# Another order of the first phase, and 28 products that nothing reads, in a kernel of attention and a two-layer FFN

## The chip, the cores and the metric

One core of a Trainium2 chip runs the kernel. The time is that of the device for one execution, in microseconds (us). The engines are TensorE (PE; its weight loads stand apart as PEld), VectorE (DVE), ScalarE (ACT), GpSimd (POOL) and SyncE (SP, which here issues all the DMAs).

## What is computed

```
attention, for each of 8 batches and 8 heads (576 positions, 64 wide):
  q_d, k_d, v_d = means over 4 neighbouring positions          # 144 positions
  out_d   = softmax(q_d k_d^T / 8) v_d                          # pooled part
  scores  = q k^T / 8 where |i - j| < 4, else -1e9
  out     = repeat(out_d, 4) + softmax(scores) v                # local part
x = out as 4608 tokens x 512
h = x w_in                                                       # 512 x 2048
g = h where h >= 1;  0 where h <= -1;  (h + 1)^2 / 4 between
result = g w_out                                                 # 2048 x 512
```

## The kernel before

**Work units.** Attention goes by pairs of heads, four pairs to a batch: pair n is one run of the generator `attention(n, pool)`, cut by `yield` into nine pieces. For a pair, PE makes the local scores (`sl_ps`, L179 and L191) and the pooled scores (`sp_ps`, L226); DVE takes maxima (L210, L242, L243) and subtracts (L211); ACT makes the exponentials, `sl` in place at L218 and `sp` in three parts at L246; DVE sums, inverts and scales both in place (L255 to L261); PE transposes them (`tl_ps` L280, `tp_ps` L292); ACT copies these out (`al`, `ap`); PE multiplies by v (`pl_ps` L324, L336); ACT and DVE put the two parts together (`xd` L345, `x` L347), and ACT and POOL split x into a rounded part `xh` (L358) and its rest `xl` (L359).

**The FFN** takes 512 tokens (`c`) and 128 hidden columns (`f`) at a time. `mm1` makes `h_ps` in 12 products (L463) and the activation behind it (`u`, `gh`, `gl`); `mm2` adds 12 products to four `o_ps` banks (L499). There are 9 x 16 such steps of each. The weights arrive as 512 KB blocks (`raw_i`, `raw_o`), and `convert_weights` (step `c`) makes each of them usable: two passes on ACT (L381, L383), two on DVE (L386, L387, both into `m`), a rounding on ACT (L389) and a subtraction on POOL (L390).

**Order.** Two tables are written out by hand. `BEFORE_STEPS` runs the first batch (pairs 0 to 3, and the first pieces of pair 4's loads); then `FIRST_STEPS` mixes the FFN's first steps (`s` is an `mm1`, `m` an `mm2`) with pairs 4 to 7; a loop does the rest. In a table `a2` is the next piece of pair 2, `q3` loads pair 3's q and k, `v` loads the first v, `w` loads one block of w_in and one of w_out, and `c` converts one block. A scheduler turns this order into one queue for each engine, which the engine works off in order, with waits on semaphores.

**Buffers.** While the first batch runs, four PSUM tiles of two banks go round over all of `sl_ps`, `sp_ps`, `tl_ps`, `tp_ps` and `pl_ps`; from pair 4 on there is one. `sl` has two buffers. Ten products of an identity matrix by itself (`warm`, L433) stand at the very start.

## Time and profile before

| | |
|---|---|
| median of 3 runs | 999.39 us (997.0 to 999.83) |
| the profiled execution | 999.97 us |
| its span on the chip | 998.2 us |
| PE busy | 966.9 us, 97% |
| DVE / ACT / POOL busy | 389.2 / 456.4 / 370.0 us |
| mean granted clock of TensorE | 0.978 |

The span runs from the first to the last instruction; the 1.8 us between it and the execution's time lie around it. [...]

### The profile page before, as it was taken

The page shows a single profiled execution, that of the slowest core. Times are in us where ns is not written, and L with a number is a line of the kernel's source. Part 1 is how long each engine was busy: PE and PEld are TensorE (multiplying, and loading weights), DVE is VectorE, ACT ScalarE, POOL GpSimd, SP SyncE. Part 2 cuts the span into 40 slices and gives each one's busy share as a digit, 9 for nine tenths or more (in the row PEclk, how much of TensorE's full clock was granted, in tenths as well). Part 3 has the DMA queues.
Part 4 walks back from the last instruction along what each step waited for, and adds up shares of the span by engine and source line. Part 5 has one row for each costly group of instructions (what it writes and reads, how often), then busy time and mean ns, then how long its engine had stood idle before and what let it go on. Part 6 is the DMA issues. An engine that isn't in the chain of part 4 may idle for free.

```text
span 998.2 us, 16966 instructions
## 1 busy us (share of the span) xinstructions
PE 966.9 (97%) x7036; PEld 765.2 (77%) x7036; DVE 389.2 (39%) x644; ACT 456.4 (46%) x911; POOL 370.0 (37%) x309
## 2 busy tenths in 40 slices
PE   5699999999999999999999999999999999999998
PEld 4577777777777777777777777777777788888886
DVE  5978795333333333333333333333333311111110
ACT  3889444444454444443443444444444443334333
POOL 1556665333333333333333333333333322222222
PEclk7679999999999999999999999999999999999999
DMA  8695111211121112111121112111211010001001
GB/s 292 222 325 167 51 49 50 83 34 50 50 91 40 35 50 92 49 50 50 62 80 49 29 48 92 49 41 36 89 50 50 14 43 0 1 1 43 1 1 42
DMA packets 26524, 66.13 MB, mean 66 GB/s; under 512 B 3152, under 2 KB 3152, under 8 KB 26448
## 3 DMA queue, kind: packets, MB, share of 16 engines
q1 hardware_dynamic: 26448, 65.06, 20.2%
q8 instruction: 55, 0.90, 0.4%
q14 instruction: 21, 0.17, 0.1%
HBM read 55.61 MB, written 9.44 MB: 65 GB/s over the span
## 4 chain that ended last, share of the span: by engine, by line
PE 86%; DVE 5%; issue 3%; ACT 2%; POOL 2%; DMA 1%; SPq 0%; POOLq 0%; DVEq 0%; ACTq 0%
PE o_ps L499 37%; PE h_ps L463 37%; PE sl_ps L191 2%; PE pl_ps L324 2%; PE tp_ps L292 2%; PE pl_ps L336 2%; PE sp_ps L226 2%; PE tl_ps L280 2%; DVE m L386 1%; DVE m L387 1%; POOL gl L485 1%; DMA raw_o<-w_out 1%; ACT sp L246 1%; DMA vp_sb<-vp 1%; DVE vd L268 0%
## 5 line engine op out<-in xcount | busy, mean ns | idle before, releaser
L463 PE MATMUL h_ps<-xh,w_i 128*128 128x512 f32 x1152 | 374.2, 402 | 0.0
L499 PE MATMUL o_ps<-w_o,gh 128*128 128x512 f32 x1152 | 360.9, 394 | 0.1
L485 POOL TENSOR_TENSOR gl<-u,gh 128x512 fp32r<-128x512 f32 x144 | 187.3, 1301 | 435.7 <-ACT gh L484 326.2
L481 DVE SCALAR_TENSOR_TENSOR u<-h_ps,u 128x512 f32<-128x512 f32 x144 | 99.5, 691 | 452.9 <-ACT u L480 449.9
L499 PEld LDWEIGHTS o_ps<-w_o,gh 128*128 128x128 f32 x1152 | 215.7, 188 | 48.5 <-issue 0.8
L463 PEld LDWEIGHTS h_ps<-xh,w_i 128*128 128x128 f32 x1152 | 211.5, 189 | 48.3 <-issue 5.4
L499 PE MATMUL o_ps<-w_o,gl 128*128 128x512 f32 x576 | 229.4, 398 | 2.7 <-POOL gl L485 2.7
L463 PE MATMUL h_ps<-xl,w_i 128*128 128x512 f32 x576 | 227.0, 394 | 0.0
L479 ACT ACTIVATE u<-h_ps 128x512 f32<-128x512 f32 x128 | 75.9, 593 | 148.1 <-PE h_ps L463 148.1
L484 ACT CAST gh<-u 128x512 fp32r<-128x512 f32 x144 | 89.5, 622 | 107.0 <-DVE u L481 106.9
L499 PEld LDWEIGHTS o_ps<-w_o,gl 128*128 128x128 f32 x576 | 108.1, 188 | 33.2 <-issue 4.5
L463 PEld LDWEIGHTS h_ps<-xl,w_i 128*128 128x128 f32 x576 | 108.5, 188 | 24.1
L480 ACT ACTIVATE u<-u 128x512 f32<-128x512 f32 x128 | 80.9, 632 | 3.9
L273 POOL TENSOR_TENSOR vh<-vp_sb 72x512 f32<-72x512 f32 x28 | 36.8, 1313 | 113.2 <-ACT u L480 91.5
L218 ACT ACTIVATE sl<-sl 128x640 f32<-128x640 f32 x32 | 23.6, 738 | 104.9 <-POOL sl L217 104.9
L246 ACT ACTIVATE sp<-sp_ps,mxp 128x144 f32<-128x144 f32 x96 | 36.5, 381 | 35.0 <-DVE mxp L244 33.2
L359 POOL TENSOR_TENSOR xl<-x,xh 128x576 fp32r<-128x576 f32 (+2 forms) x40 | 47.5, 1197 | 6.3 <-ACT xh L358 6.3
L217 POOL TENSOR_TENSOR sl<-sl,mxl 128x640 f32<-128x640 f32 x28 | 35.5, 1268 | 31.1 <-DVE mxl L216 31.1
L284 ACT COPY al<-tl_ps 128x640 f32<-128x640 f32 x32 | 22.2, 694 | 52.7 <-PE tl_ps L280 52.7
L255 DVE TENSOR_REDUCE sp_ps<-sl 128x10 f32<-128x640 f32 x32 | 26.5, 827 | 42.3 <-ACT sp L246 42.2
L213 DVE TENSOR_TENSOR sl<-sl_ps,band_sb 128x640 f32<-128x640 f32 x28 | 23.0, 823 | 38.3 <-PE sl_ps L191 38.3
L280 PE MATMUL tl_ps<-ident,sl 128*128 128x128 f32 x160 | 25.4, 292 | 12.9 <-DVE sl L258 11.7
(67 smaller groups left out, 765.5 us busy)
## 6 DMA issues: line engine op xcount, KB each, us to landing
v_sb<-vw SPq DMA_DIRECT2D x32, 320.0 KB, 5.3
vp_sb<-vp SPq DMA_DIRECT2D x32, 288.0 KB
out<-osb SPq DMA_DIRECT2D x36, 256.0 KB, 2.2
raw_i<-w_in SPq DMA_DIRECT2D x16, 512.0 KB, 7.2
raw_o<-w_out SPq DMA_DIRECT2D x16, 512.0 KB, 6.0
q_sb<-qT SPq DMA_DIRECT2D x28, 288.0 KB, 3.1
k_sb<-kT SPq DMA_DIRECT2D x28, 288.0 KB, 7.8
first_i<-qT SPq DMA_DIRECT2D x4, 288.0 KB
```

The source lines that it names most:

```text
L217: nc.gpsimd.tensor_tensor(slf, slf, ml_n, op=ALU.subtract)
L246: nc.scalar.activation(sp[:, i], sp_v[:, i] if i < 2 else sp_w, AF.Exp, bias=mx[:, i : i + 1], scale=scale, accum_out=sums[:, NB + i : NB ...
L273: nc.gpsimd.tensor_tensor(vh, vpt[:, :, 0:2, :], vpt[:, :, 2:4, :], op=ALU.add)
L280: nc.tensor.transpose(tl_v[:, g * P : (g + 1) * P], sl[:, g].rearrange("p r c -> p (r c)"), ident)
L359: nc.gpsimd.tensor_tensor(xl[:, p, dst], x[:, part], xh[:, p, dst], op=ALU.subtract)
L463: nc.tensor.matmul(h[:, :TCH], wi[:, wt, cc * P : (cc + 1) * P], xt[:, cc, ts], start=(n == 0), stop=(n == 3 * NCC - 1),)
L479: nc.scalar.activation(u, h[:, :TCH], AF.Relu, bias=0.5, scale=0.5)
L480: nc.scalar.activation(u, u, AF.Square)
L481: nc.vector.scalar_tensor_tensor(u, h[:, :TCH], 1.0, u, op0=ALU.max, op1=ALU.min)
L484: nc.scalar.copy(gh, u)
L485: nc.gpsimd.tensor_tensor(gl, u, gh, op=ALU.subtract)
L499: nc.tensor.matmul(o, gt[:, ts], wo[:, wt, :], start=f == 0 and n == 0, stop=f == NFC - 1 and n == 2)
```

## The change

Both tables are replaced, and a helper `keep_clock` puts products of a tile by the identity matrix on PE, for the first four pairs only: two on the local scores before their exponential, two behind it, and one behind each of the three pooled exponentials, so 7 to a pair and 28 in all. Their results go to parts of the `sl_ps` and `sp_ps` tiles that nothing reads. Lines of the changed kernel have higher numbers from there on (L218 is L232 there, L246 is L261, L386 is L402, L463 is L479); the products stand on L164.

```diff
--- before.py
+++ after.py
@@ -70,6 +70,8 @@
 
 WARM = 10
 
+FILL = 2
+
 PIECES = (3, 4, 2, 1)
 
 
@@ -77,13 +79,13 @@
 
 
 BEFORE_STEPS = """
-    q0 v q1 a0 a0 a0 a0 a1 q2 a1 a0 a1 a0 w a1 a2 q3 a0 a2 a1 a2 a0 c a1 a0 a2 w a3 c a1
-    a3 a2 a0 a3 a1 c a2 a1 a3 w a2 c a3 a1 a2 a3 c a2 w a3 c a2 a3 c a3 c a3
+    q0 v q1 a0 a0 a0 a0 a1 q2 a1 a0 a0 a1 a2 w a1 w q3 c a2 a1 a1 a0 a2 a0 a0 a3 a2 c a1
+    a3 a2 a0 a3 a1 c a2 a1 a3 a2 c a3 w a1 a2 c w a3 c a2 a3 a3 a2 c a3 c a3
 """.split()
 FIRST_STEPS = """
-    a4 a4 a4 s a4 a4 w a4 s a4 a4 w a4 c m c s a4 w m c c s a5 a5 m w c c a5 s a5 a5 m w
-    c c a5 s a5 a5 a5 m w c s a5 m c w c c s a6 a6 m w a6 s c c a6 a6 m a6 w s c c a6 a6
-    a6 m w s c c a6 s m w c c a7 a7 m a7 s w c c a7 a7 m a7 s c c a7 a7 a7 m s a7 m s m
+    a4 a4 a4 a4 s a4 a4 w a4 a4 s a4 m c c a4 w s w m c a5 c s a5 a5 m w c c s a5 a5 m w
+    c c s m a5 a5 a5 a5 w c w s a5 c m c s c w a6 a6 m a6 s c c a6 a6 m w a6 s c c a6 a6
+    w m w s c a6 c a6 s m c a7 a7 m a7 s w c c a7 a7 m a7 s c a7 a7 m c s a7 m c s a7 m
 """.split()
 
 
@@ -151,6 +153,15 @@
         if n < NPAIR and n % 2:
             return wpool.tile(shape, F32, name=f"{name}_{n}", tag=second[tag])
         return apool.tile(shape, F32, name=name, tag=tag, bufs=1)
+
+    def keep_clock(n, out, data, count=FILL):
+
+
+
+
+        if n < NPAIR:
+            for _ in range(count):
+                nc.tensor.matmul(out, ident, data, start=True, stop=True)
 
     def attention(n, pool):
 
@@ -215,7 +226,11 @@
             )
             nc.vector.tensor_reduce(ml, slf, axis=AX.X, op=ALU.max)
             nc.gpsimd.tensor_tensor(slf, slf, ml_n, op=ALU.subtract)
+
+        rest = sl_ps[:, 0, 0:SL0]
+        keep_clock(n, rest, sl[:, 0].rearrange("p r c -> p (r c)"))
         nc.scalar.activation(slf, slf, AF.Exp, scale=0.125)
+        keep_clock(n, rest, sl[:, 0].rearrange("p r c -> p (r c)"))
         yield
         sp_ps = pool.tile([P, 2, 512], F32, name="sp_ps", tag="a")
         sp_v = sp_ps[:, 0, 0 : 2 * SD].rearrange("p (n s) -> p n s", n=2)
@@ -251,6 +266,7 @@
                 scale=scale,
                 accum_out=sums[:, NB + i : NB + i + 1],
             )
+            keep_clock(n, sp_ps[:, 1, 2 * SD : 3 * SD], sp[:, i], 1)
         yield
         nc.vector.tensor_reduce(sums[:, 0:NB], slf, axis=AX.X, op=ALU.add)
         nc.vector.tensor_scalar_add(sums, sums, 1e-9)
```

What stands in the engines' queues, with the semaphores that each row waits for:

PE, from the pooled scores of pair 1 to the transposes of pair 0, before (names ending in 88, 90 are q and k of pairs 1, 2; `DVE_49`, `Activation_49` and so on are waits for that engine):

```order
L226 MATMUL sp_ps<-kd_156,qd_153 64x144 [waits DVE_49,PE_49]
L226 MATMUL sp_ps<-kd_156,qd_153 64x144 x5
L179 MATMUL sl_ps<-band_r,ident_r 128x384 [waits DVE_49,PE_49]
L179 MATMUL sl_ps<-band_r,ident_r 128x256
L191 MATMUL sl_ps<-first_o_90,first_i_89 64x64 [waits DMAHW7_49,DMAHW0_49]
L191 MATMUL sl_ps<-first_o_90,first_i_89 64x64 x19
L280 MATMUL tl_ps<-ident,sl 128x128 [waits DVE_49]
L280 MATMUL tl_ps<-ident,sl 128x128 x4
```

The same place in the changed kernel (L164 are the added products, L202 and L241 what L191 and L226 were):

```order
L241 MATMUL sp_ps<-kd_160,qd_157 64x144 [waits PE_49]
L241 MATMUL sp_ps<-kd_160,qd_157 64x144 x4
L164 MATMUL sl_ps<-sl,ident 128x128 [waits Activation_49]
L164 MATMUL sl_ps<-sl,ident 128x128
L164 MATMUL sp_ps<-sp,ident 128x144 [waits Activation_49]
L241 MATMUL sp_ps<-kd_160,qd_157 64x144
L190 MATMUL sl_ps<-band_r,ident_r 128x384 [waits PE_49]
L190 MATMUL sl_ps<-band_r,ident_r 128x256
L202 MATMUL sl_ps<-first_o_90,first_i_89 64x64 [waits DMAHW7_49,DMAHW0_49]
L202 MATMUL sl_ps<-first_o_90,first_i_89 64x64 x8
L164 MATMUL sp_ps<-sp,ident 128x144 [waits Activation_49]
L164 MATMUL sl_ps<-sl,ident 128x128 [waits DVE_49]
```

The added products on pair 0's exponentials stand ahead of the scores of pair 2 and inside them, and each waits for ACT or DVE.

ACT, from its first weight block to the pooled exponentials of pair 1, before:

```order
L381 ACTIVATE raw_i_207<-raw_i_207 128x512 [waits DMAHW2_49]
L383 ACTIVATE raw_i_207<-raw_i_207 128x512
L381 ACTIVATE raw_o_209<-raw_o_209 128x512 [waits DMAHW3_49]
L218 ACTIVATE sl<-sl 128x640 [waits DVE_49]
L383 ACTIVATE raw_o_209<-raw_o_209 128x512
L246 ACTIVATE sp,sp_ps<-sp_ps,mxp 128x144 [waits DVE_49,PE_49]
L246 ACTIVATE sp,sp_ps<-sp_ps,mxp 128x144 [waits Activation_49] x2
L218 ACTIVATE sl<-sl 128x640 [waits DVE_49]
```

The same place in the changed kernel (L232 and L261 are the local and the pooled exponentials, L397 and L399 the two passes over a weight block):

```order
L397 ACTIVATE raw_i_221<-raw_i_221 128x512 [waits DMAHW2_49]
L399 ACTIVATE raw_i_221<-raw_i_221 128x512
L397 ACTIVATE raw_o_223<-raw_o_223 128x512 [waits DMAHW3_49]
L399 ACTIVATE raw_o_223<-raw_o_223 128x512
L232 ACTIVATE sl<-sl 128x640 [waits DVE_49,PE_49]
L261 ACTIVATE sp,sp_ps<-sp_ps,mxp 128x144 [waits DVE_49]
L397 ACTIVATE raw_i_232<-raw_i_232 128x512 [waits DMAHW4_49]
L399 ACTIVATE raw_i_232<-raw_i_232 128x512
L261 ACTIVATE sp,sp_ps<-sp_ps,mxp 128x144 [waits PE_49]
L397 ACTIVATE raw_o_234<-raw_o_234 128x512 [waits DMAHW5_49]
L261 ACTIVATE sp,sp_ps<-sp_ps,mxp 128x144 [waits PE_49]
L399 ACTIVATE raw_o_234<-raw_o_234 128x512
L232 ACTIVATE sl<-sl 128x640 [waits DVE_49,PE_49]
```

Five more passes over weight blocks stand ahead of the local exponential of pair 1, and the exponentials wait for PE.

DVE, around the output x of pair 1 (`x_492`, here `x_520`) and the scaling of pair 3's local weights (L258, here L274), before:

```order
L386 TENSOR_SCALAR m<-raw_i_462 128x512 [waits DMAHW3_49,Pool_49]
L386 TENSOR_SCALAR m<-raw_o_464 128x512 [waits DMAHW4_49,Pool_49]
L387 ISA m<-raw_i_462,m 128x1024 [waits DVE_49]
L387 ISA m<-raw_o_464,m 128x1024 [waits DVE_49]
L255 TENSOR_REDUCE sp_ps<-sl 128x10 [waits Activation_49]
L386 TENSOR_SCALAR m<-raw_i_551 128x512 [waits DMAHW5_49,Pool_49]
L256 TENSOR_SCALAR sp_ps<-sp_ps 128x13 [waits DVE_49]
L387 ISA m<-raw_i_551,m 128x1024 [waits DVE_49]
L257 RECIPROCAL sp_ps<-sp_ps 128x13 [waits DVE_49]
L347 TENSOR_TENSOR x_492<-pl_ps,xd_490 128x576 [waits Activation_49]
L258 TENSOR_TENSOR sl<-sl,sp_ps 128x640 [waits DVE_49]
L261 TENSOR_TENSOR sp_482<-sp_482,sp_ps 128x432
```

The same place in the changed kernel (L402 and L403 are the two passes into m):

```order
L402 TENSOR_SCALAR m<-raw_i_514 128x512 [waits DMAHW3_49,Pool_49]
L402 TENSOR_SCALAR m<-raw_o_516 128x512 [waits DMAHW4_49,Pool_49]
L403 ISA m<-raw_i_514,m 128x1024 [waits DVE_49]
L403 ISA m<-raw_o_516,m 128x1024 [waits DVE_49]
L402 TENSOR_SCALAR m<-raw_i_541 128x512 [waits DMAHW5_49,Pool_49]
L402 TENSOR_SCALAR m<-raw_o_543 128x512 [waits DMAHW6_49,Pool_49]
L403 ISA m<-raw_i_541,m 128x1024 [waits DVE_49]
L363 TENSOR_TENSOR x_520<-pl_ps,xd_518 128x576 [waits Activation_49]
L403 ISA m<-raw_o_543,m 128x1024 [waits DVE_49]
L271 TENSOR_REDUCE sp_ps<-sl 128x10 [waits PE_49]
L177 TENSOR_REDUCE first_qd<-q_sb 128x144 [waits DMAHW1_49]
L272 TENSOR_SCALAR sp_ps<-sp_ps 128x13 [waits DVE_49]
```

Before, six passes into m stand here ahead of x, and two behind; now seven stand ahead of x and one behind, and the sums of pair 3 (L255, here L271) have moved behind x.

## Rows read from the trace of the kernel before

**Rows 1.** The page: the granted clock of TensorE over the span in 40 equal slices, in tenths.

```profile
PEclk7679999999999999999999999999999999999999
```

**Rows 2.** Busy time of each engine, in us and with the number of instructions (PE, PEld, DVE, ACT, POOL), then granted clock, DMA share and GB/s, in stretches cut where the granted clock changes, and in a long one behind them.

```profile
13.20:26.70 13.50, 6.59 (x93) 5.50 (x95) 9.09 (x19) 9.71 (x25) 2.06 (x3) 0.50 0.97 341
26.90:30.20 3.30, 0.90 (x24) 0.57 (x16) 3.30 (x5) 3.30 (x8) 2.86 (x3) 1.00 0.53 145
30.30:37.00 6.70, 5.89 (x65) 4.50 (x65) 5.56 (x12) 3.76 (x9) 3.08 (x3) 0.50 0.99 383
37.10:40.40 3.30, 0.00 (x0) 0.00 (x0) 3.23 (x9) 3.30 (x10) 1.06 (x1) 1.00 0.96 382
40.50:60.90 20.40, 16.80 (x212) 13.27 (x213) 16.91 (x23) 16.93 (x36) 13.99 (x12) 0.50 0.52 161
...
165.00:900.00 735.00, 735.00 (x5365) 581.62 (x5365) 247.35 (x423) 316.75 (x637) 256.87 (x216) 1.00 0.16 49
```

**Rows 3.** PE in order of time until the FFN's first product: start, length, instruction, number of records (a product of float32 operands has two); in brackets PE's idle time before it and what ended it.

```profile
1.41 4.64 PE L433 MATMUL warm<-ident 128*128 128x128 f32 x20 [1.41 <-POOL ident masks.py:199]
...
15.67 0.87 PE L179 MATMUL sl_ps<-band_r,ident_r 128*128 128x384 f32 x2 [4.18 <-DVE sl L211]
...
22.45 1.33 PE L280 MATMUL tl_ps<-ident,sl 128*128 128x128 f32 x5 [4.43 <-DVE sl L258]
...
31.04 1.30 PE L280 MATMUL tl_ps<-ident,sl 128*128 128x128 f32 x5 [3.24 <-DVE sl L258]
...
40.94 0.66 PE L280 MATMUL tl_ps<-ident,sl 128*128 128x128 f32 x2 [4.01 <-DVE sl L258]
...
49.88 1.33 PE L280 MATMUL tl_ps<-ident,sl 128*128 128x128 f32 x5
51.00 1.49 PE L292 MATMUL tp_ps<-ident,sp 128*72 128x128 f32 x6
54.31 0.36 PE L191 MATMUL sl_ps<-k_sb,q_sb 64*64 64x64 f32 x1 [1.82 <-DVE x L347]
...
58.39 1.22 PE L463 MATMUL h_ps<-xh,w_i 128*128 128x512 f32 x2
```

**Rows 4.** PE in order of time with the FFN running.

```profile
62.51 0.71 PE L226 MATMUL sp_ps<-kd,first_qd 64*64 64x144 f32 x12
63.15 0.74 PE L463 MATMUL h_ps<-xh,w_i 128*128 128x512 f32 x2
...
66.03 0.63 PE L499 MATMUL o_ps<-w_o,gh 128*128 128x512 f32 x2
...
73.03 0.71 PE L280 MATMUL tl_ps<-ident,sl 128*128 128x128 f32 x5
...
74.97 0.81 PE L292 MATMUL tp_ps<-ident,sp 128*72 128x128 f32 x6
```

**Rows 5.** ACT in order of time, at its first weight blocks.

```profile
14.87 0.67 ACT L381 ACTIVATE raw_i<-raw_i 128x512 f32<-128x512 f32 x1 [11.96 <-DMA raw_i<-w_in]
...
16.70 0.68 ACT L381 ACTIVATE raw_o<-raw_o 128x512 f32<-128x512 f32 x1 [0.60 <-DMA raw_o<-w_out]
17.28 0.72 ACT L218 ACTIVATE sl<-sl 128x640 f32<-128x640 f32 x1
...
19.70 0.74 ACT L218 ACTIVATE sl<-sl 128x640 f32<-128x640 f32 x1
```

**Rows 6.** DVE in order of time: sums (L255) and scaling (L258) of local weights, passes into m, and the output x of pair 1.

```profile
19.84 0.83 DVE L255 TENSOR_REDUCE sp_ps<-sl 128x10 f32<-128x640 f32 x1 [4.32 <-ACT sp L246]
...
21.57 0.82 DVE L258 TENSOR_TENSOR sl<-sl,sp_ps 128x640 f32<-128x640 f32 x1
...
27.68 2.49 DVE L386 TENSOR_SCALAR m<-raw_o 128x512 int32<-128x512 int32 x1
30.09 0.81 DVE L258 TENSOR_TENSOR sl<-sl,sp_ps 128x640 f32<-128x640 f32 x1
...
42.06 0.41 DVE L386 TENSOR_SCALAR m<-raw_o 128x512 int32<-128x512 int32 x1
...
43.00 0.68 DVE L387 CUSTOM_DVE_ANT_0 m<-raw_o,m 128x1024 uint16<-128x1024 uint16 x1
...
44.82 1.73 DVE L387 CUSTOM_DVE_ANT_0 m<-raw_i,m 128x1024 uint16<-128x1024 uint16 x1
...
46.63 0.73 DVE L347 TENSOR_TENSOR x<-pl_ps,xd 128x576 f32<-128x576 f32 x1
47.28 0.80 DVE L258 TENSOR_TENSOR sl<-sl,sp_ps 128x640 f32<-128x640 f32 x1
```

**Rows 7.** POOL in order of time, while DVE's pass of 27.68 us stood.

```profile
27.34 1.30 POOL L273 TENSOR_TENSOR vh<-vp_sb 72x512 f32<-72x512 f32 x1 [11.58 <-PE pl_ps L324]
28.60 1.28 POOL L390 TENSOR_TENSOR w_i<-m,w_i 128x512 fp32r<-128x512 f32 x1
```

**Rows 8.** What PE waited for between 58 and 215 us: us in total, times, longest.

```profile
PE o_ps L499 <- POOL gl L485: 2.3, 3, 1.4
PE tl_ps L280 <- DVE sp L261: 1.2, 2, 0.9
PE pl_ps L324 <- ACT ap L298: 0.9, 2, 0.5
PE sl_ps L191 <- DVE x L347: 0.4, 1, 0.4
```

## Prediction

> **What bounds the kernel now.** I read the windows first. From 165 to 900 us PE is busy in all of 735.00 us, at a granted clock of 1.00 [rows 2]; nothing there waits, so a microsecond won or lost before 165 us reaches the end whole. The page's clock row shows where something can be won: it is below full only in the first three slices of 25 us [rows 1]. Cut at its changes, the first 61 us have three stretches at 0.50, with 6.59, 5.89 and 16.80 us of PE work in them, 29.3 together, and between them two short stretches at 1.00 in which PE does 0.90 us and nothing [rows 2]. So the upper level comes mostly when PE has no work for it.
>
> PE in order of time then shows that this phase isn't PE's. It stands idle 4.18, 4.43, 3.24 and 4.01 us ahead of the groups at 15.67, 22.45, 31.04 and 40.94, each time for DVE's subtraction or scaling [rows 3]. The FFN's first product starts at 58.39. Four lines of waits are left behind it, 2.3 + 1.2 + 0.9 + 0.4 = 4.8 us [rows 8]. What the change can move is the 58.39, the level at which the FFN begins, and the 4.8.
>
> **The added products.** None stands in the trace of before. The nearest row is the ten of L433, 4.64 us, so 0.46 us for a 128-column product, run before anything else [rows 3]. The transpose of the same shape takes 1.33 us for five at 0.50 and 0.71 at 1.00 [rows 3, 4], so I take half, 0.23 us, at the upper level, and 144/128 of both for the 144-column ones: 16 x 0.46 + 12 x 0.52 = 13.6 us at 0.50, 6.8 at 1.00. In front of PE's idle time they are hidden. They are not hidden where someone waits: the local exponential works in place and must wait for the two products that read its input, the scaling for the two behind it, and in the order each next pooled exponential waits for PE as well.
>
> PE takes its queue in order, and the trace shows it: the scores at 54.31 end a wait for x, and what stands behind them starts behind them [rows 3]. [...] By this rule an added product whose exponential is late stops the real scores behind it, which speaks against the change.
>
> **The new order, station by station.** I lay the rows of the new order end to end, each starting when its engine is free and its last releaser done.
>
> ACT: the DMAs ahead of the first two weight blocks are as they were, so ACT takes them up at 14.87 and 16.70 [rows 5]. Both passes over the second block (0.57 each) now precede pair 0's local exponential: 17.8 instead of 17.28. Then come the first pooled one, two passes on w_in 1, the second, a pass on w_out 1, the third, one more pass, and pair 1's local exponential. Four passes are 2.3 us; the second and third wait for an added product, the third for one that has two band products and nine score products ahead of it. Pair 1's exponential comes to about 23.3 instead of 19.70 [rows 5].
>
> DVE: pair 0's sums move from 19.84 to 23.6, and with nine short rows between, its scaling from 21.57 to 26.1 [rows 6]. Pair 1's stays near 30.2 (30.09 before): in the old order a pass into m stood just ahead of it and took 2.49 us, where one alone takes 0.41 [rows 6], because POOL was in two products of its own until 29.88 [rows 7]; in the new one that pass falls in a pause of POOL. Pair 2's comes out unchanged.
>
> Then seven passes into m stand in one block ahead of x of pair 1. They start at 41.0, behind pair 2's scaling and one row more. Alone they are 4 x 0.41 + 3 x 0.68 = 3.7 us [rows 6]. POOL has four rows to do there, and a pass beside one costs 1.05 (1.73 instead of 0.68) to 2.08 us more [rows 6]; I take three such passes at 1.05, 3.2 us (0 and 3 x 2.08 are the ends). x of pair 1 moves from 46.63 to 47.9. Behind it stand x itself, the last pass, the sums, a reduction and two short rows, 3.2 us in all: pair 3's scaling moves from 47.28 to 51.1.
>
> The trace also shows a wait longer than one POOL row: the pass that came at 27.68 ended behind POOL's second row, not its first at 28.64 [rows 6, 7]. [...] By the row at 27.68 one of the passes waits a second time, 1.3 us, and the sum is that much higher.
>
> PE from pair 3's scaling on: transposes start at 52.0, and 1.12 + 1.43 of them, 15 scores of pair 4 (1.0), pair 3's last products (2.4) and five scores (0.3) bring it to 58.3 at 0.50, 55.2 at 1.00. The pooled scores of pair 4 now come before the first FFN product and wait for DVE to read the single score tile, to 58.7; they take 0.64 (62.51 to 63.15 [rows 4]). First FFN product: 59.3, **+0.9**.
>
> **The sum**, against the profiled execution's 999.97 us. First product +0.9. The pooled scores of pair 4, done by then, -0.64. The first twelve products took from 58.39 to 62.51, 4.12 us, where the next took from 63.15 to 66.03, 2.88 [rows 3, 4]; from 52.0 PE has hardly a pause, as it had before the level rose at 60.9, so I take the upper level for all twelve: -1.24 (0 to -1.24). The waits behind: the first table gives pair 4 a piece more before the first `mm1` and puts two of these closer together, so the wait for gl shrinks; of 4.8 I take -0.5 (all of it gone and as much again are the ends, -4.8 to +4.8). The sum is -1.5: 998.5, and as the profiled execution lies 0.6 above the median, **997.9** for the median. The 28 products cost nothing in it beyond the station at 23.3: the cover is PE's idle time between 11 and 41 us, four stretches of 15.9 us in all before [rows 3], against products of 6.8 to 13.6; if that cover goes, it is the second rival.
>
> **The rivals.**
>
> *The level holds to the FFN* (faster). If the added products keep PE at 1.00 through 47 to 58 too, the chain from 52.0 is 3.1 us shorter, less 0.2 for the wait on DVE's read. First product 56.4 instead of 59.3: 997.9 - 2.9 = 995.0. For it: the level rose at 26.8 and 37.1, each time behind PE work without a pause, from 22.45 and from 31.04 on [rows 2, 3]. Against it: at 30.2 and 40.5 it fell again, while PE was idle ahead of 31.04 and 40.94, and the block of seven passes leaves PE idle some 3 us at 46 to 49, with no added product to put there. [...]
>
> *The products run at the lower level* (slower). At 0.50 they are 13.6 us of work in PE's one queue; with the 29.3 that were there PE is nearly full from 13 to 60. A pair's seven then take 3.3 us instead of 1.7 between its scores and its scaling; four pairs make 6.6, of which I take half as hidden under DVE and ACT: +3.3, and the FFN begins at 0.50, +1.24: 997.9 + 4.5 = 1002.4. It decides from the point where the products no longer fit into PE's idle time and their excess passes 3 us. A second POOL row per blocked pass, 1.3, would bring 1003.7. [...]
>
> *The new order alone matters.* Without effect of the products on the level, the order has the +3.6 at the front and the block of seven against one stall of 2.08 avoided: within 1.5 us of the old, so no change. This belongs to the forecast.
>
> **Chances.** A time within 0.3% (3 us, about what a measurement of this kernel can tell from no change), by the forecast or by the order alone: 0.45. The level held: 0.33. The lower level: 0.22. The forecast's own range is 996.4 to 1001. To hold 8 in 10 it reaches to the faster case with 2 us more of the waits gone, 993, and to the slower with the second POOL row, 1003.7.
>
> **What would show it.** In the changed trace: pair 1's local exponential near 23 us; pair 0's scaling near 26, pair 3's near 51; x of pair 1 near 48 behind a block of passes into m with some over 1 us; the granted clock at 1.00 through most of 23 to 45, lower around 47 to 57, full at the first FFN product at 59.3; waits behind it of 4 to 5 us. The prediction is wrong if the first product starts before 57.5 or behind 61, if the clock stays at 0.50 from 13 to 60, or if the waits behind it move by more than 2 us.

## Result and the profile after

The changed kernel takes **1008.62 us** (median of 4, 1006.43 to 1009.43) beside 999.61 for the kernel before (median of 4): ratio 1.0091, 95% interval 1.0071 to 1.0111, so 9 us slower. The forecast was 997.9, its range ended at 1003.7. Run again later (e15 below) it took 1005.11 (1001.73 to 1007.03), ratio 1.0056 (1.0041 to 1.0071): slower both times, by amounts that differ, and the experiments show why they can. One execution each of e1, e4 and e13 below was far longer (3958.75, 1200.77 and 1039.73 us); the medians hold it and move by 0.4 us at most without it, the ratios leave it out.

The profiled execution took 1006.43 us, its span 1004.6. It is the fastest of the four: the two profiles differ by 6.4 us (spans of 1004.6 and 998.2) where the medians differ by 9, and no profile here shows the rest. The first view is that of [rows 2]: busy time, granted clock and traffic in stretches, here cut at the clock changes of the kernel after.

```profile
12.08:32.56 20.48, 15.71 (x114) 11.94 (x117) 10.61 (x22) 10.38 (x26) 3.37 (x4) 0.50 0.73 262
32.56:46.21 13.65, 10.23 (x148) 7.30 (x141) 13.29 (x24) 12.46 (x28) 7.44 (x6) 1.00 0.78 272
46.21:49.62 3.41, 3.41 (x53) 2.68 (x53) 3.41 (x8) 2.64 (x5) 0.88 (x1) 0.50 0.08 30
49.62:56.45 6.83, 3.52 (x62) 2.61 (x60) 6.83 (x3) 3.34 (x9) 6.68 (x6) 1.00 0.83 280
56.45:63.28 6.83, 3.68 (x54) 3.15 (x58) 6.71 (x10) 5.28 (x10) 2.21 (x2) 0.50 0.23 92
63.28:104.24 40.96, 37.00 (x306) 28.27 (x300) 33.18 (x49) 36.74 (x76) 23.79 (x18) 1.00 0.71 252
104.24:107.65 3.41, 3.41 (x9) 2.64 (x9) 3.22 (x8) 2.80 (x6) 1.37 (x2) 0.50 0.00 0
165.00:900.00 735.00, 734.60 (x5407) 580.53 (x5406) 251.87 (x429) 318.45 (x640) 261.29 (x219) 1.00 0.16 49
```

From 165 us on PE is busy all the time but 0.4 us, nearly as in [rows 2]. Before the FFN the clock is at 1.00 for longer, and with work in it: between 32.56 and 56.45 PE is busy 13.75 us at 1.00, where [rows 2] has 0.90. The clock is lifted, and the kernel is slower all the same.

PE in order of time, as [rows 3]:

```profile
25.46 1.22 PE L164 MATMUL sl_ps<-sl,ident 128*128 128x128 f32 x4
26.48 0.69 PE L164 MATMUL sp_ps<-sp,ident 128*128 128x144 f32 x2
...
32.84 0.71 PE L164 MATMUL sl_ps<-sl,ident 128*128 128x128 f32 x4
33.49 0.55 PE L340 MATMUL pl_ps<-al,v_sb 64*64 64x58 f32 x18
...
59.60 1.33 PE L296 MATMUL tl_ps<-ident,sl 128*128 128x128 f32 x5 [5.92 <-DVE sl L274]
...
66.52 0.74 PE L479 MATMUL h_ps<-xh,w_i 128*128 128x512 f32 x2
...
103.26 0.50 PE L515 MATMUL o_ps<-w_o,gl 128*128 128x512 f32 x1 [1.90 <-POOL gl L501]
```

The FFN's first product starts at 66.52, 8.13 later than the 58.39 of [rows 3]; ahead of it PE waits 5.92 us for pair 3's scaling. From the first product to the end of the span it is 938.1 us, where it was 939.8. So the loss is all ahead of 66.52, and it is DVE's scaling that is late. DVE and POOL show where (as [rows 6, 7]; L271 are the sums, L274 the scaling, L403 the second pass into m, L363 x; L406 and L375 are POOL's subtractions for the weights and for `xl`):

```profile
24.74 0.83 DVE L271 TENSOR_REDUCE sp_ps<-sl 128x10 f32<-128x640 f32 x1 [3.21 <-PE sp_ps L164]
...
27.18 0.81 DVE L274 TENSOR_TENSOR sl<-sl,sp_ps 128x640 f32<-128x640 f32 x1
...
29.96 0.83 DVE L271 TENSOR_REDUCE sp_ps<-sl 128x10 f32<-128x640 f32 x1 [1.46 <-PE sp_ps L164]
...
32.99 0.81 DVE L274 TENSOR_TENSOR sl<-sl,sp_ps 128x640 f32<-128x640 f32 x1
...
45.16 0.82 DVE L274 TENSOR_TENSOR sl<-sl,sp_ps 128x640 f32<-128x640 f32 x1
...
50.68 0.74 DVE L363 TENSOR_TENSOR x<-pl_ps,xd 128x576 f32<-128x576 f32 x1
51.34 5.58 DVE L403 CUSTOM_DVE_ANT_0 m<-raw_o,m 128x1024 uint16<-128x1024 uint16 x1
56.85 0.81 DVE L271 TENSOR_REDUCE sp_ps<-sl 128x10 f32<-128x640 f32 x1
...
58.72 0.82 DVE L274 TENSOR_TENSOR sl<-sl,sp_ps 128x640 f32<-128x640 f32 x1
```

```profile
50.28 1.06 POOL L290 TENSOR_TENSOR vd<-vh 72x256 f32<-72x256 f32 x1
51.30 1.27 POOL L406 TENSOR_TENSOR w_i<-m,w_i 128x512 fp32r<-128x512 f32 x1
52.52 1.28 POOL L406 TENSOR_TENSOR w_o<-m,w_o 128x512 fp32r<-128x512 f32 x1
53.75 1.41 POOL L375 TENSOR_TENSOR xl<-x,xh 128x576 fp32r<-128x576 f32 x1
55.11 1.27 POOL L406 TENSOR_TENSOR w_i<-m,w_i 128x512 fp32r<-128x512 f32 x1
57.66 1.28 POOL L406 TENSOR_TENSOR w_o<-m,w_o 128x512 fp32r<-128x512 f32 x1 [1.28 <-ACT w_o L405]
```

Two things stand out. The scalings of pairs 0, 1 and 2 come 5.6, 2.9 and 5.2 us later than before (21.57 and 30.09 [rows 6], and 39.98), and two of the sums end a wait for L164, an added product. And one pass into m, 0.68 us alone, took 5.58: it began at 51.34, 0.04 behind a row of POOL, and ended 0.54 behind the end of POOL's fourth row, the first that no other followed at once. Pair 3's sums stand behind it.

### The profile page after: what moved, and what is told of

Same layout as the page of the kernel before. It is cut to its first block, busy times and chain, and to the rows that moved or that the text cites. A ratio compares the mean times of both kernels' runs of the same rounds, so it can differ in the third digit from the quotient of the medians.

```text
span 1004.6 us, 17074 instructions
## 1 busy us (share of the span) xinstructions
PE 976.2 (97%) x7092; PEld 771.4 (77%) x7092; DVE 390.9 (39%) x644; ACT 457.9 (46%) x911; POOL 368.6 (37%) x309
## 4 chain that ended last, share of the span: by engine, by line
PE 85%; issue 5%; DVE 4%; POOL 2%; DMA 2%; ACT 1%; SPq 0%; POOLq 0%; DVEq 0%; ACTq 0%
PE h_ps L479 36%; PE o_ps L515 36%; PE sl_ps L202 3%; PE pl_ps L340 2%; PE tp_ps L308 2%; PE pl_ps L352 2%; PE sp_ps L241 2%; POOL gl L501 2%; PE tl_ps L296 2%; DVE m L403 1%; DVE m L402 1%; DMA raw_o<-w_out 1%; DMA vp_sb<-vp 0%; PE sl_ps L164 0%; PE sp_ps L164 0%
## 5 line engine op out<-in xcount | busy, mean ns | idle before, releaser
L479 PE MATMUL h_ps<-xh,w_i 128*128 128x512 f32 x1152 | 373.4, 401 | 0.0
L497 DVE SCALAR_TENSOR_TENSOR u<-h_ps,u 128x512 f32<-128x512 f32 x144 | 99.5, 691 | 452.5 <-ACT u L496 450.3
L479 PEld LDWEIGHTS h_ps<-xh,w_i 128*128 128x128 f32 x1152 | 211.0, 188 | 48.0 <-issue 5.0
L479 PE MATMUL h_ps<-xl,w_i 128*128 128x512 f32 x576 | 226.6, 393 | 0.7 <-POOL xl L375 0.7
L479 PEld LDWEIGHTS h_ps<-xl,w_i 128*128 128x128 f32 x576 | 108.4, 188 | 25.2 <-POOL xl L375 1.1
L232 ACT ACTIVATE sl<-sl 128x640 f32<-128x640 f32 x32 | 23.6, 739 | 103.8 <-POOL sl L228 103.3
L261 ACT ACTIVATE sp<-sp_ps,mxp 128x144 f32<-128x144 f32 x96 | 36.6, 381 | 40.6 <-DVE mxp L259 34.0
L375 POOL TENSOR_TENSOR xl<-x,xh 128x576 fp32r<-128x576 f32 (+2 forms) x40 | 47.3, 1189 | 3.5 <-ACT xh L374 3.4
L271 DVE TENSOR_REDUCE sp_ps<-sl 128x10 f32<-128x640 f32 x32 | 26.4, 826 | 41.7 <-ACT sp L261 37.0
L374 ACT CAST xh<-x 128x576 fp32r<-128x576 f32 (+2 forms) x40 | 22.4, 578 | 25.0 <-DVE x L363 24.9
```

What stands on the lines that cost most here:

```text
L261: nc.scalar.activation(sp[:, i], sp_v[:, i] if i < 2 else sp_w, AF.Exp, bias=mx[:, i : i + 1], scale=scale, accum_out=sums[:, NB + i : NB ...
L375: nc.gpsimd.tensor_tensor(xl[:, p, dst], x[:, part], xh[:, p, dst], op=ALU.subtract)
L479: nc.tensor.matmul(h[:, :TCH], wi[:, wt, cc * P : (cc + 1) * P], xt[:, cc, ts], start=(n == 0), stop=(n == 3 * NCC - 1),)
L497: nc.vector.scalar_tensor_tensor(u, h[:, :TCH], 1.0, u, op0=ALU.max, op1=ALU.min)
```

## The experiments

All ran beside runs of the kernel before; the ratio is to these. The three columns on the right are starts in each profile (before: 39.98, 47.28, 58.39); a profile is of one execution, which can lie some us from the median (e3's took 999.77 us, e4's 1002.40). The lines of the code have other numbers in some of them: the second pass into m is L401 to L409, the scaling L272 to L275.

| kernel | median, us | ratio (95%) | pair 2's scaling | pair 3's | first FFN product |
|---|---|---|---|---|---|
| the change | 1008.62 | 1.0091 (1.0071 to 1.0111) | 45.16 | 58.72 | 66.52 |
| e15 the change again | 1005.11 | 1.0056 (1.0041 to 1.0071) | 44.41 | 55.37 | 64.83 |
| e1 order only | 997.88 | 0.9988 (0.9977 to 0.9998) | 40.09 | 48.09 | 57.10 |
| e2 products only | 1000.68 | 1.0025 (1.0013 to 1.0036) | 42.73 | 51.88 | 59.52 |
| e3 products of identity | 1002.86 | 1.0036 (1.0023 to 1.0049) | 42.95 | 52.94 | 59.78 |
| e4 one conversion later | 1004.15 | 1.0051 (1.0035 to 1.0066) | 45.73 | 55.22 | 62.67 |
| e5 block 3 in one row | 1004.12 | 1.0057 (1.0044 to 1.007) | 45.37 | 55.37 | 63.05 |
| e6 all blocks in one row | 1005.93 | 1.0072 (1.0059 to 1.0085) | 49.45 | 56.98 | 66.20 |
| e7 local products only | 998.67 | 0.9996 (0.9988 to 1.0005) | 40.35 | 50.62 | 58.19 |
| e8 pooled products only | 1002.17 | 1.0031 (1.0019 to 1.0043) | 43.82 | 54.96 | 62.64 |
| e9 pooled behind the third | 1002.71 | 1.0033 (1.0023 to 1.0044) | 40.94 | 53.06 | 61.04 |
| e10 e7, block 3 later | 1002.61 | 1.0028 (1.0018 to 1.0039) | 40.50 | 47.57 | 57.01 |
| e11 old order, local products | 1000.80 | 1.0016 (1.0008 to 1.0025) | 40.71 | 50.98 | 58.97 |
| e12 e1, block 3 later | 999.91 | 1.0008 (0.9999 to 1.0017) | 38.35 | 44.34 | 53.76 |
| e13 pooled behind the scaling | 1008.97 | 1.0096 (1.0081 to 1.011) | 43.07 | 55.44 | 68.11 |
| e14 e9 and e5 together | 998.32 | 0.9992 (0.9984 to 1.0001) | 42.22 | 51.60 | 59.51 |
| e16 e1, one conversion later | 997.99 | 0.9982 (0.9973 to 0.9992) | 38.84 | 46.50 | 55.73 |

### The order alone, the products alone

e1 (the new tables, no product):

```diff
     def keep_clock(n, out, data, count=FILL):
-        if n < NPAIR:
-            for _ in range(count):
-                nc.tensor.matmul(out, ident, data, start=True, stop=True)
+        return
```

> The changed kernel with its two new tables, and none of the 28 products. Theory C (the collision): most of the loss is one pass into m (line 403, block 3 of w_out) that stands ahead of pair 3's sums and took 5.58 us there instead of 0.68, beside four POOL rows without a gap; the new order puts it there, so it stays without the products: 1003 to 1007, the pass 3 us or more. Theory P (the products): the 28 products hold up the exponentials and so the scalings of pairs 0 to 2, which came 5.6, 2.9 and 5.2 us later than before; without them the order costs nothing: 998 to 1001, pair 3's scaling at 47 to 51.

e2 is the other half, the products with both tables of before:

```diff
 BEFORE_STEPS = """
-    q0 v q1 a0 a0 a0 a0 a1 q2 a1 a0 a0 a1 a2 w a1 w q3 c a2 a1 a1 a0 a2 a0 a0 a3 a2 c a1
+    q0 v q1 a0 a0 a0 a0 a1 q2 a1 a0 a1 a0 w a1 a2 q3 a0 a2 a1 a2 a0 c a1 a0 a2 w a3 c a1
...
```

> The kernel before with its own two tables, and the 28 products added. Theory C (the collision): the old order has no run of four POOL rows beside a pass ahead of pair 3's sums, so the products cost only what they hold up at the front: 999 to 1002. Theory P (the products): they cost here what they cost in the changed kernel, 1004 to 1009, with the scalings of pairs 0 and 1 late by 3 us or more.

Neither reproduces the loss: 1.1 us faster by the order, 1.7 slower by the products, 9 slower by both. In e1 the time is 0.1 us under P's range and far from C's, in e2 it is in C's and far from P's. As each stood, both fall: it takes the order and the products together. In e1 the pass is there, but hardly held.

```profile
46.38 1.02 DVE L401 CUSTOM_DVE_ANT_0 m<-raw_o,m 128x1024 uint16<-128x1024 uint16 x1
...
48.09 0.80 DVE L272 TENSOR_TENSOR sl<-sl,sp_ps 128x640 f32<-128x640 f32 x1
```

It took 1.02 us and pair 3's scaling came at 48.09. Against e1, the first product of the change is 9.42 later: 5.07 at pair 2's scaling, 5.56 from there to pair 3's (13.56 against 8.00 us, of which the pass is 4.56), and 1.21 given back from there on (7.80 against 9.01), where the clock is higher (1.00 from 63.28 on; in e1 0.50 up to the first product).

### Which products

e7 leaves out the call behind the pooled exponentials:

```diff
-            keep_clock(n, sp_ps[:, 1, 2 * SD : 3 * SD], sp[:, i], 1)
```

e8 leaves out the two calls on the local scores instead:

```diff
-        keep_clock(n, rest, sl[:, 0].rearrange("p r c -> p (r c)"))
         nc.scalar.activation(slf, slf, AF.Exp, scale=0.125)
-        keep_clock(n, rest, sl[:, 0].rearrange("p r c -> p (r c)"))
```

> The changed kernel without the 12 products behind the pooled exponentials; the 16 on the local scores stay. If the waits of the pooled exponentials for PE (2.11, 1.09 and 0.94 us, one behind another) make the front late: pair 0's scaling at 24 to 25 instead of 27.18, pair 2's at 41 to 43, and the meeting with the POOL run may go: 999 to 1004. If the local products make it late: 1005 to 1009.

> The changed kernel without the 16 products on the local scores; the 12 behind the pooled exponentials stay. The counterpart of the run before: if the pooled products make the front late, pair 0's scaling stays at 26 to 27 and the time at 1003 to 1009; if the local ones do, 997 to 1001.

Without the 12 pooled products the time is that of before (e7, a little under its range). Alone they leave it 3.2 us above, between e8's two ranges: neither kind makes the whole loss without the other. e11 puts the 16 local products alone into the old order (e2 with e7's edit):

> The kernel before with its own tables and the 16 local products alone, without the 12 pooled ones. Theory W: the local products cost next to nothing here either (e7 against e1: 0.8 us): 998 to 1000.5, against 1000.68 with all 28. Theory P: 1000 to 1002.

There they take as long as all 28 in e2 (1000.80 and 1000.68): 0.3 above W's range and inside P's, and the 12 pooled ones cost nothing more that these runs can tell (ratios 1.0016 and 1.0025, with intervals that overlap). So the price is not one of the products as such; it hangs on what stands around them.

e3 makes all of them of the identity matrix, so that they read nothing that is being made:

```diff
-                nc.tensor.matmul(out, ident, data, start=True, stop=True)
+                nc.tensor.matmul(out[:, 0:P], ident, ident, start=True, stop=True)
```

> The changed kernel, with each of the 28 products made of the identity matrix by itself (128 columns each, into the same parts of the score tiles), so that none reads sl or sp and no exponential waits for one. Theory C: DVE's order around pair 3 stays, so the collision can stay: 1003 to 1007, if the pass again meets a POOL run. Theory P in the form that the waits of the exponentials cost the time: 2.1 + 0.4 + 1.1 + 0.9 us of ACT's waits for line 164 go, 1003 to 1005 with the collision and 998 to 1000 without. Theory P in the form that the products' own time on PE costs it: no change, 1007 to 1009.

It came out just under C's lower bound, which is also the lower bound of P's first form, and the waits did not go:

```profile
21.53 0.38 ACT L261 ACTIVATE sp<-sp_ps,mxp 128x144 f32<-128x144 f32 x1 [1.66 <-PE sp_ps L164]
...
23.52 0.83 DVE L271 TENSOR_REDUCE sp_ps<-sl 128x10 f32<-128x640 f32 x1 [3.21 <-PE sp_ps L164]
```

Ahead of the first FFN product ACT still waits 3.5 us in all, and DVE's sums 3.9, for L164 into `sp_ps`. What ties them is the tile that is written. The second and third exponentials read `sp_ps` and the sums write into it, so each waits for the product that writes a part of it that nobody reads; the sums stand in the other half of the tile, and wait all the same.

### The place of the 12 pooled products

e9 has all 28 products, with a pair's three pooled ones behind its third exponential:

```diff
-            keep_clock(n, sp_ps[:, 1, 2 * SD : 3 * SD], sp[:, i], 1)
+        for i in range(NQB):
+            keep_clock(n, sp_ps[:, 1, 2 * SD : 3 * SD], sp[:, i], 1)
         yield
```

> The changed kernel with all 28 products and both new tables; only the place of the 12 pooled products is changed: a pair's three stand behind its third pooled exponential instead of one behind each. Theory W (the products cost little as work; what costs is that the second and third exponential each wait for the product ahead of them, and the sums for the last): ACT's 4.5 us of waits for line 164 behind pooled exponentials go, pair 0's scaling comes at 24 to 25.5 instead of 27.18, pair 2's at 42 to 44 instead of 45.16, and the time is 999 to 1003. Theory P (their work on PE costs the time): 1006 to 1009.

The same work on PE in another place: 1002.71 instead of 1008.62 (1005.11 in e15), in theory W's range. Pair 2's scaling came at 40.94, better than expected, pair 0's at 26.37, worse: the sums still wait 2.8 us for the last of the three. Pair 3's was 53.06 for another reason:

```profile
48.12 1.21 DVE L403 TENSOR_SCALAR m<-raw_o 128x512 int32<-128x512 int32 x1
49.37 3.01 DVE L404 CUSTOM_DVE_ANT_0 m<-raw_o,m 128x1024 uint16<-128x1024 uint16 x1
...
53.06 0.80 DVE L275 TENSOR_TENSOR sl<-sl,sp_ps 128x640 f32<-128x640 f32 x1
```

Two passes held by POOL, 3.1 us more than alone, stand between the sums and the scaling.

e13 moves them behind the scaling, where nobody waits for them:

```diff
             sp, sp, sums[:, NB:].unsqueeze(2).broadcast_to([P, NQB, SD]), op=ALU.mult
         )
+        for i in range(NQB):
+            keep_clock(n, sp_ps[:, 1, 2 * SD : 3 * SD], sp[:, i], 1)
```

> The changed kernel with all 28 products and both tables; a pair's three pooled products stand behind its scaling, where neither an exponential nor a sum waits for them. Theory W (waits for the 12 products, and the meeting with POOL that the lateness leads to, are the whole loss; their work on PE is hidden): as e7 without them, 997.5 to 1001, pair 2's scaling at 40 to 42 and pair 3's at 48 to 52. Theory P (what is left in e9, 3.6 us, is their work on PE): 1001.5 to 1004, as e9. If a pass into m is again held over several POOL rows ahead of pair 3's scaling, the time is 1 us higher for each.

Both theories missed: 1008.97. PE in order of time, and the pass:

```profile
51.54 0.68 PE L341 MATMUL pl_ps<-al,v_sb 64*64 64x61 f32 x30 [2.33 <-DVE x L364]
56.82 1.81 PE L164 MATMUL sp_ps<-sp,ident 128*128 128x144 f32 x6 [4.59 <-DVE sp L276]
58.56 0.67 PE L341 MATMUL pl_ps<-al,v_sb 64*64 64x58 f32 x10
```

```profile
51.56 3.96 DVE L403 TENSOR_SCALAR m<-raw_o 128x512 int32<-128x512 int32 x1
55.44 0.81 DVE L273 TENSOR_TENSOR sl<-sl,sp_ps 128x640 f32<-128x640 f32 x1
```

Nobody waits for the products, but they wait: pair 3's three stand in the middle of pair 2's last products (30 records ahead of them, 10 behind) and wait 4.59 us for a scaling that a held pass made late. Pair 2's last ten products, whose input `al` ACT had copied out by 46.61, start at 58.56. Held up in PE's queue, the wait is as dear here as on ACT.

### The held pass

e4 moves the conversion of block 3 of w_out from the end of the first table behind the first `s` of the second:

```diff
-    a3 a2 a0 a3 a1 c a2 a1 a3 a2 c a3 w a1 a2 c w a3 c a2 a3 a3 a2 c a3 c a3
+    a3 a2 a0 a3 a1 c a2 a1 a3 a2 c a3 w a1 a2 c w a3 c a2 a3 a3 a2 c a3 a3
...
-    a4 a4 a4 a4 s a4 a4 w a4 a4 s a4 m c c a4 w s w m c a5 c s a5 a5 m w c c s a5 a5 m w
+    a4 a4 a4 a4 s c a4 a4 w a4 a4 s a4 m c c a4 w s w m c a5 c s a5 a5 m w c c s a5 a5 m w
```

> The changed kernel with one step moved: the last c of the first table (block 3 of w_out) comes behind the first s of the second. Its pass into m is then behind pair 4's pooled maxima instead of ahead of pair 3's sums; the pass that stands ahead of the sums is that of block 3 of w_in. Theory C, a pass is held over as many POOL rows as follow each other without a gap: POOL has three rows in a run there instead of four, as the fourth is block 3 of w_in's own, so the scaling comes 1.3 to 5.5 us earlier: 1003 to 1007. Rival: a pass is held over one POOL row at most and the 5.58 us were something else: no change to the pass's place, so 1007 to 1009 or, where the pass costs 1.3 at most, 1002 to 1004.

The pass that now stands there (block 3 of w_in) met POOL rows with a pause of 0.66 us after the second and took 2.34 us: it stood over two rows, which the rival excludes. The time, 1004.15, is in C's range. But the pause is POOL's wait for ACT's `xh`, not the shorter run that C counted on, and the time is also near what the change itself took in e15, so that it tells little here.

e5 makes the two blocks numbered 3 by one DVE row each:

```diff
+        if f == 3:
+            nc.vector.scalar_tensor_tensor(
+                mi, t[:, :, 1], 3, t[:, :, 0], op0=ALU.logical_shift_left, op1=ALU.bitwise_or
+            )
+        else:
             nc.vector.tensor_scalar(mi, t[:, :, 1], 3, None, op0=ALU.logical_shift_left)
             nc.vector.tensor_tensor(mi, mi, t[:, :, 0], op=ALU.add)
```

> The changed kernel, in which the two weight blocks numbered 3 alone are made usable by one DVE row each (a shift and a bitwise or, 128x512, in the form of the activation's row L497, which took 0.69 us beside POOL) instead of the two passes of lines 402 and 403; where the low part rounds up to 8 a carry is lost. DVE's rows up to there are the same. Theory C (the pass that meets the POOL run is the last and largest part of the loss): pair 3's scaling comes at 52 to 53.5 instead of 58.72, the first FFN product at 60 to 61.5 instead of 66.52, and the time is 1001.5 to 1004. Rival: any DVE row that reads and writes SBUF is held by the POOL run in the same way: 1006 to 1009. Rival: something else would have held pair 3's transposes anyway: the scaling comes at 53 but the first product stays behind 64, 1005 to 1008.

In e5 no held pass is left between x of pair 1 (50.82) and the scaling, and the time is 1004.12, just above its range. Of the 5.2 to 6.7 us expected at the scaling 3.4 came (55.37 for 58.72):

```profile
49.10 1.79 DVE L403 SCALAR_TENSOR_TENSOR m<-raw_o 128x512 int32<-128x512 int32 x1
50.82 0.74 DVE L363 TENSOR_TENSOR x<-pl_ps,xd 128x576 f32<-128x576 f32 x1
51.48 0.74 DVE L177 TENSOR_REDUCE first_qd<-q_sb 128x144 f32<-128x576 f32 x1
54.01 0.83 DVE L271 TENSOR_REDUCE sp_ps<-sl 128x10 f32<-128x640 f32 x1 [1.79 <-PE sp_ps L164]
```

Where the pass had been, the sums now wait for the pooled products, till 54.01. The pass had covered that wait. In time e5 is no better than the change was in e15 (ratios 1.0057 and 1.0056); it is the rows that tell. And the new form is held too: 1.79 us instead of 0.69, ahead of x. e6 uses it for every block (`if True` in the same diff):

> The changed kernel with all 32 weight blocks made usable by one DVE row each as in the run before. Theory C: no row is held by POOL any more, and 0.4 us less per block before pair 2's scaling: the late scaling of pair 2 (45.16) comes at 41 to 43, the first FFN product at 57 to 60, the time 998 to 1001.5. Theory P (the products cost their time through PE, whatever DVE does): the scalings of pairs 0 and 1 stay at 27 and 33, and the time stays above 1002.

In e6 theory C's expectation fell, and the signs named for P came (pair 0's scaling at 27.39, pair 1's at 33.70, the time above 1002). But the rows show both causes at full size: 1005.93, with 4.32 us of waiting for L164 ahead of pair 3's sums, and a one-row pass of 4.50 us:

```profile
37.04 4.50 DVE L403 SCALAR_TENSOR_TENSOR m<-raw_i 128x512 int32<-128x512 int32 x1
```

The activation's row of the same form (L497), with one operand in PSUM, took 0.69 us at most, beside POOL rows too.

e14 takes away both causes: e9's place and e5's rows.

> e9 and e5 in one kernel: the 12 pooled products behind the third pooled exponential, and weight block 3 by one DVE row each. e5 alone took 4.5 us off the changed kernel, e9 alone 5.9 of its 9. If the late exponentials and the held pass are two causes: 998.5 to 1000.5. If the held pass is only a consequence of the lateness, already gone in e9 but for 2.3 us: 1000 to 1002.5.

998.32, a little under its range and 1.1 us under before, with all 28 products on PE; e15 beside it on the same chip took 1005.11. e9 alone had left 3.6 us and e5 alone 5.1 above before, so the two causes together carry the whole loss in time. (The one-row form is also shorter by itself, 0.69 us where two passes take 1.09; e14 does not separate this from the held passes.) The first FFN product is still 1.1 us later than in [rows 3] (59.51); behind it 938.4 us follow, not 939.8.

e15 is the change itself once more, beside e13 and e14:

> The changed kernel itself once more, beside e13 and e14 and with a profile of its own. If the meeting of the pass with POOL is a property of the program and not of one execution: again a pass of block 3 of w_out over 5 us at 51 us and a first FFN product at 66 to 67, 1006 to 1010. If it is chance which of the two engines goes first: another length of that pass, by steps of 1.25 us, and the time lower by as much.

The same program met POOL otherwise this time:

```profile
50.58 2.99 DVE L403 CUSTOM_DVE_ANT_0 m<-raw_o,m 128x1024 uint16<-128x1024 uint16 x1
```

```profile
50.54 1.26 POOL L406 TENSOR_TENSOR w_i<-m,w_i 128x512 fp32r<-128x512 f32 x1
51.77 1.25 POOL L406 TENSOR_TENSOR w_o<-m,w_o 128x512 fp32r<-128x512 f32 x1
53.31 1.54 POOL L375 TENSOR_TENSOR xl<-x,xh 128x576 fp32r<-128x576 f32 x1 [0.29 <-ACT xh L374]
```

POOL paused 0.29 us ahead of its third row, and in this pause the pass went through, 2.59 us shorter: two steps of the second expectation. So its length is a matter of some tenths on other engines. Of the 3.35 us by which pair 3's scaling came earlier than in the first profile, 1.69 were left at the first FFN product: the clock stayed at 0.50 all the way there, and the stretch took 9.46 us instead of 7.80. The time of this kernel lies between 1001.7 and 1009.4.

### Block 3 later

e10 (on e7) and e12 (on e1) move both conversions of block 3 behind the first `s`:

```diff
-    a3 a2 a0 a3 a1 c a2 a1 a3 a2 c a3 w a1 a2 c w a3 c a2 a3 a3 a2 c a3 c a3
+    a3 a2 a0 a3 a1 c a2 a1 a3 a2 c a3 w a1 a2 c w a3 c a2 a3 a3 a2 a3 a3
...
-    a4 a4 a4 a4 s a4 a4 w a4 a4 s a4 m c c a4 w s w m c a5 c s a5 a5 m w c c s a5 a5 m w
+    a4 a4 a4 a4 s c c a4 a4 w a4 a4 s a4 m c c a4 w s w m c a5 c s a5 a5 m w c c s a5 a5 m w
```

e16 moves that of w_out alone: e4's edit, on e1.

> The changed kernel without the 12 pooled products (as in e7), and with the two conversions of weight block 3 moved behind the first s of the second table, so that no pass into m stands between x of pair 1 and pair 3's scaling. In e7 two passes held by POOL (1.19 and 1.82 us) stand there, and two more just ahead. If these are what is left: pair 3's scaling at 47 to 48.5 instead of 50.62, the first FFN product at 55 to 56.5 instead of 58.19, the time 995.5 to 998. Rival: block 3 then comes late for the fourth step of the FFN, and the wait is only moved: 998 to 1001.

> The new tables without any product (as in e1), and the two conversions of block 3 moved as in e10. If the passes ahead of pair 3's scaling cost what they last, the scaling comes at 46 to 47 instead of 48.09 and the first FFN product at 55 to 56 instead of 57.10: 996 to 997.5. The difference to e10 is what the 16 local products do for the clock between pair 3's scaling and the FFN: 7.6 us in e7 against 9.0 in e1, so e10 is 0 to 1.4 us the faster one if that alone counts.

> The new tables without any product (e1), with the conversion of block 3 of w_out alone moved behind the first s of the second table. In e12, with both conversions moved, the first FFN product came 3.3 us earlier than in e1 (53.76) but the time was 2 us longer. If block 3 of w_in is what the FFN then waits for: here 995.5 to 997.5. If any conversion moved there costs later what it saves here: 998 to 1000.

In e10 and e12 pair 3's scaling came as early as expected (in e12 earlier still), but the times missed, in e10 both ranges: what was won ahead of the first product was given back behind it. From there to the end it takes 944.5 us in e10 and 938.5 in e7, 943.7 in e12 and 940.8 in e1; in e12 PE waits there 1.7 us for x (ending at 80.55) and 1.6 for scalings, which e1 does not have. e16 came out between its two ranges: 997.99, ratio 0.9982 (0.9973 to 0.9992), 1.8 us better than before by the ratio, with none of the 28 products. e1 has 0.9988 (0.9977 to 0.9998), so it is not shown that the moved conversion adds to what the order alone gives.

## Why the prediction was wrong

**What bounds it: right.** Ahead of 165 us alone something could move, and a microsecond lost there reached the end.

**The products' price and cover: roughly right.** Two 128-column products take 1.02 us from start to start at 0.50 (25.46 to 26.48) and 0.65 at 1.00 (32.84 to 33.49): 0.51 and 0.32 each, where I had 0.46 and 0.23. PE is busy 37.95 us between 13 us and the first FFN product instead of 27.87, 10 more though at a higher mean clock (0.72 for 0.58); the rows of L164 alone are busy 13.6 us of it. So the 28 took 10 to 13.6 us, within my 6.8 to 13.6. e14 (998.32 us with all 28) shows that they hide in PE's idle time, as the sum had it; the rival of the lower level, which let their work spill over, was not the mechanism.

**ACT's station: right, in part by luck.** Pair 1's local exponential came at 23.56 (I had 23.3). Pair 0's came at 17.07, 0.7 us ahead of my 17.8, and the way from there took 1.0 longer; the two errors cancelled.

**DVE's stations: the step that failed.** I followed the waits of the pooled exponentials for pair 0 only. There I was 1.1 us short (27.18, not 26.1), since I left out that the sums wait for the last product as well. Then I wrote that pair 1's scaling "stays near 30.2" and pair 2's "comes out unchanged". The same chain (exponential, product, exponential, product, and so on to the sums) stands in pair 1 too, and its scaling came at 32.99. Pair 2's came at 45.16, 5.2 us later than the 39.98 that I had kept. There no pooled exponential waits for L164: the lateness is carried on. Against e1, the same order without the products, the scalings of pairs 0, 1 and 2 are 4.1, 5.0 and 5.1 us late, so all but 0.1 of it arises in the first two pairs; and e9, where only the place of the pooled products differs, has pair 2's at 40.94. In ACT's rows the chain is plain to see (L232 are the local exponentials of pairs 0 and 1; the first L261 is the last of pair 0's, the other three are pair 1's):

```profile
17.07 0.72 ACT L232 ACTIVATE sl<-sl 128x640 f32<-128x640 f32 x1
...
22.69 0.38 ACT L261 ACTIVATE sp<-sp_ps,mxp 128x144 f32<-128x144 f32 x1 [2.11 <-PE sp_ps L164]
...
23.56 0.74 ACT L232 ACTIVATE sl<-sl 128x640 f32<-128x640 f32 x1
...
25.66 0.38 ACT L261 ACTIVATE sp<-sp_ps,mxp 128x144 f32<-128x144 f32 x1 [0.86 <-DVE mxp L259]
...
27.20 0.38 ACT L261 ACTIVATE sp<-sp_ps,mxp 128x144 f32<-128x144 f32 x1 [1.09 <-PE sp_ps L164]
...
28.58 0.38 ACT L261 ACTIVATE sp<-sp_ps,mxp 128x144 f32<-128x144 f32 x1 [0.94 <-PE sp_ps L164]
```

Three exponentials of 0.38 us take from 25.66 to 28.96, with a trip to PE's queue between each two. The rows of the queues ahead of the prediction show the products with a wait for ACT; what waits for them in turn I had followed for one pair.

**The block of passes: mis-sized.** The block of seven took 4.3 us (46.42 to 50.68), less than my 6.9. The one behind it, which I counted at its own length within 3.2 us of rows, took 5.58. I weighed [rows 6, 7] and held to one POOL row for a pass, with a second at 1.3 us as an addition to a rival: 1003.7 was the end of my range by that. It was four. Pair 2's 5.2 us and the pass's 4.9, less the block's 2.6, make 7.5 of the 7.6 by which pair 3's scaling (58.72) missed my 51.1; the first product, at 66.52, is far behind the 61 that I had named as the sign of being wrong. The traces show which rows were held: the second pass (5.58 us here) and the one-row form (4.50 in e6), both with two inputs in SBUF, and the first pass, with one (3.96 in e13); and, in the first 260 us of the 18 traces, none of 150 rows of x that met a POOL row, which have an operand in PSUM (0.76 us at the longest), nor of 158 reductions of k (0.77). That a waiting pass gets through behind one POOL row was my assumption. No run shows it as a limit: the pass of 2.49 us in [rows 6] ended behind POOL's second row [rows 7], this one behind the fourth.

**The clock: half right.** It was to be 1.00 in most of 23 to 45; it was so from 32.56. Around 47 to 57 it was to be low: it was at 0.50 from 46.21 to 49.62 and again from 56.45, and at 1.00 for the 6.83 us between. At the first product it was full, as I had it. From pair 3's scaling to the first product the change takes 7.80 us, near the 8.2 of my own stations (51.1 to 59.3) and far from the 5.3 of the rival of the held level (51.1 to 56.4). Before takes 11.11, but e1, without a product, 9.01, so that 2.1 of the 3.3 us gained come with the order and 1.2 with the products; and in e15, at 0.50 up to the first product, these 1.2 were not there (9.46). What the products gain through the clock in this stretch is small and does not come every time.

**Behind the first product: right in sign.** I had -2.4 us there (0.64, 1.24 and 0.5), the profiles show -1.7. What PE waited for from the first product to 215 us, as [rows 8]:

```profile
PE o_ps L515 <- POOL gl L501: 1.9, 1, 1.9
PE pl_ps L340 <- ACT ap L314: 1.2, 3, 0.4
PE h_ps L479 <- POOL xl L375: 0.7, 1, 0.7
```

That is 3.8 us in all, 1.0 less than before and just under the 4 to 5 that I had named; but the one wait of 1.9 is followed by 3.41 us at 0.50 (first table), which before does not have.

**The order alone** was forecast within 1.5 us of before: e1, -1.1.

## What to carry to other kernels

An instruction whose result nobody reads can still cost (here 1008.62 us with the 28 products and 997.88 in e1 without them), through what waits for it and through what stands behind it while it waits itself: follow, in every repetition and not only the first, who uses the tiles that it reads and writes, and what stands behind it in its own queue. A DVE row that is held beside POOL (here 0.68 us alone and 5.58 beside four rows) must be placed by POOL's pauses, not by its own length: ahead of a row that the critical chain needs, count the whole run of POOL rows beside it as the worst case. Where one wait is taken away, look for the one that it had covered.

## What was not expected of the hardware

**A pass can be passed over again and again.** In the first 260 us of the 18 traces 340 passes into m, in either form, ran beside a POOL row and were lengthened by more than 0.04 us. 329 of them ended 0.3 to 0.6 us behind the end of the first such row; 8 stood over two rows and 3 over four (5.58, 4.50 and 3.96 us). In 120 of the 329 another POOL row followed at once, and in more than a hundred it was this row that came out longer. What decides which of the two goes first when POOL's next row is ready without a pause is open: no run here was made for it, and the same program gave four rows once and two the next time.

**The clock can fall once more in the FFN.** In the change 3.41 us at 0.50 follow the wait of 1.90 us that ended at 103.26 (first table); the first two products of an h take 0.99 us there where 0.62 to 0.63 is usual. In e1 the same follows a wait of 1.89, and nine of the 18 traces have such a fall behind their first product. Before, the longest such wait was 1.39 [rows 8] and the clock stayed at 1.00. In e10 it stayed there behind a wait of 1.75 for x, in e12 it fell behind one of 1.74 for x, so the length of the wait alone does not tell.
